# Sharing PSUM banks in the global attention: transposes four to a bank with the diagonal among them, products and splits of two query blocks together

## The chip, the core and the metric

The program runs on one core of a Trainium2 chip. The metric is device time in microseconds (us) from one execution of the whole program; less is better. TensorE is called PE, its weight loads PEld, VectorE DVE, ScalarE ACT, GpSimd POOL, and SP issues most DMAs.

## The reference

Three layers follow each other for 4 batches of 576 tokens, all in float32. First a banded attention over 8 heads (window 64, head width 64). Then a mixture of 4 attention experts, each causal over all 576 tokens, weighted by a gate that keeps 2 of the 4. Then a mixing layer with an angle, a token mix and a channel mix. The change is in the middle one:

```python
for e in range(E):                       # E = 4 experts, Hd = 64
    q = x @ wq[e]
    k = x @ wk[e]
    v = x @ wv[e]
    scores = scale * (q @ k.transpose(0, 2, 1))
    scores = np.where(causal, -1000000000.0, scores)
    scores = scores - scores.max(-1, keepdims=True)
    a = np.exp(scores)
    a /= a.sum(-1, keepdims=True) + 1e-09
    ye = a @ v @ wo[e]
    ...                                  # out += (gate weight of e) * ye
```

## The kernel before

Work is written as Python generators, one for each part: `phase_a` (banded attention of a batch), `qk` and `vg_gates` (projections and gates), `attn` (the causal attention of two experts, the part that is changed), `wo` (its output projection), `theta`, `mix`, `channel` (the last layer) and loaders of weights. `merge` interleaves a few of them by hand-set weights (the numbers in `KN`), and a scheduler then orders each engine's instructions. It works by a simulated timeline, so on an engine the order may differ from the order of emission: an instruction that is ready can come before one that was written earlier. Each engine then runs its own list strictly in that order.

`attn(b, ep)` handles batch b and the experts 2·ep and 2·ep+1, so it runs 8 times. It goes through five blocks of queries, t = 0 to 4: block 0 has 64 queries, the others have 128 each, and block t sees `QW[t]` keys. For each block it computes scores on PE (L382, L384), takes mask and maximum on DVE (L386) and exponentials on ACT (L391), and scales the weights on DVE or POOL (L403). The weights against earlier keys lie in `pn`, and those of both experts against the last 64 keys, the diagonal, side by side in `pd`. The weights are then transposed on PE, 128 columns at a time, into PSUM: up to four blocks (two key groups by two experts) into one bank `bpt` (L414), and the diagonal into a bank `bdt` of its own (L420). ACT or DVE copies each bank into the SBUF tile `pT`, called `bpT` in the profile (L416, L418 for `bpt`, L422, L424 for `bdt`; the lists `KN["BC"]` and `KN["BD"]` choose the engine). `pT` has two buffers, used in turn by successive query blocks.

The products with the values go into a third bank, `o`. Those of one expert against 128 keys (L429) have a weight tile of 64 columns and write one half of the partitions, and the two experts' halves are side by side in the array; the profile writes such a shape as `128*64`. The diagonal's product for both experts (L433) uses all 128 columns, `128*128`. A float32 product is two instructions in the trace, so block t has 4·t instructions of L429 and two of L433. Block t = 0 has only L433. `split` then moves `o` to SBUF as a high part (`oh`, a cast on ACT, L87) and a rest (`ol`, a subtraction on DVE, L90), which `wo` reads later.

The banks of `bpt`, `bdt` and `o` all come from `tbank`, two banks with the tag `tb`; in the last batch every third request goes to another tag, `ta`, with one bank. `phase_a` has products of 64 columns as well (`ao`, L260).

Of the kernel before, what the change touches and what calls it, by code (L numbers as in the profile page):

```python
# [21 lines left out]
P = 128  # L22
B, H, S, D = 4, 8, 576, 64
# [17 lines left out]
def f32(ap):  # L41
    return ap.bitcast(F32)
# [15 lines left out]
def kernel(ctx, tc, qT, kT, vw, consts, w_in, w_o, w_th, w_tk, w_ch, outT):  # L58
    nc = tc.nc
# [5 lines left out]
    ident, ma1, ma0 = (cst[:, P * i : P * i + P] for i in range(3))  # L65
# [12 lines left out]
    def bank(shape, tag, name):  # L78
        return ps.tile(shape, F32, tag=tag, bufs=BANKS[tag], name=name)
# [5 lines left out]
    def split(dst_h, dst_l, src, eng_h, eng_l):  # L85
        if eng_h is nc.scalar:
            nc.scalar.copy(out=dst_h, in_=src)  # L87
        else:
            eng_h.tensor_copy(out=dst_h, in_=src)
        eng_l.tensor_sub(out=dst_l, in0=src, in1=f32(dst_h))  # L90
# [70 lines left out]
    VD = [bp.tile([P, 5, 2, D], F32, tag=f"VD{i}", name=f"VD{i}") for i in range(2)]  # L161
# [187 lines left out]
    def tbank(b, shape, name):  # L349
        nt[0] += 1  # L350
        return bank(shape, "ta" if b == B - 1 and nt[0] % KN["TB"] == 0 else "tb", name)

    def attn(b, ep):
        vg, gw = VG[b], GW[b]
        for i in range(2):
            e = 2 * ep + i
            pool_mul(VD[ep][64 * i : 64 * i + 64, :, i, :], vg[0:64, :, e * D : (e + 1) * D], 1.0)
        oh = bp.tile([P, S], F32R, tag="oh", bufs=3, name=f"oh{b}{ep}")
        ol = bp.tile([P, S], F32R, tag="ol", bufs=3, name=f"ol{b}{ep}")
        O[b, ep] = (oh, ol)  # L360
        for t in range(5):
            w = QW[t]
            q0 = 0 if t == 0 else 64 + P * (t - 1)
            m = 64 if t == 0 else P
            mo = S - P if t == 0 else S - w
            if b == B - 1 and ep == 1 and t % 3 == 1:
                pn = rp.tile([P, 2, S], F32, tag="bmsx", name=f"bms{b}{ep}{t}")
            else:
                pn = bp.tile([P, 2, S], F32, tag="bms", bufs=2, name=f"bms{b}{ep}{t}")
            ss = sums(1, BS)  # L370
            sm = bp.tile([P, 2], F32, tag="bsm", bufs=4, name=f"bsm{b}{ep}{t}")
            pd = bp.tile([P, 2, 64], F32, tag="bpd", bufs=2, name=f"bpd{b}{ep}{t}")
            for i in range(2):
                e = 2 * ep + i
                n = f"{b}{e}{t}"
                qs, ka = QS[b, e], KA[b, e]
                ms = pn[:, i]
                cuts = [(0, w)] if w <= 512 else [(0, w // 2), (w // 2, w)]
                nm = bp.tile([P, 2], F32, tag="bnm", bufs=6, name=f"bnm{n}")
                for ci, (a, z) in enumerate(cuts):  # L380
                    s = sbank(b, [P, 512], f"bs{n}{a}")
                    nc.tensor.matmul(s[:m, : z - a], qs[:, q0 : q0 + m], ka[:, a:z],  # L382
                                     start=True, stop=False)
                    nc.tensor.matmul(s[:m, : z - a], qs[:, q0 : q0 + m], KL[e][:, a:z],  # L384
                                     start=False, stop=True)
                    nc.vector.tensor_tensor_reduce(  # L386
                        out=ms[:m, a:z], in0=s[:m, : z - a], in1=mb[:m, mo + a : mo + z],
                        scale=-0.125, scalar=nm[:m, 0:1] if ci else 3.0e38,
                        op0=ALU.add, op1=ALU.min, accum_out=nm[:m, ci : ci + 1],
                    )  # L390
                ex = nc.scalar.activation(out=ms[:m, :w], in_=ms[:m, :w], func=AF.Exp,  # L391
                                     bias=nm[:m, ci : ci + 1], scale=-1.0, accum_out=ss[:m, i, 0:1])
                if (b, ep, t, i) == (3, 1, KN["LT"], 1):
                    late[0] = ex
            nc.vector.tensor_reduce(out=sm[:m], in_=ss[:m], op=ALU.add, axis=AX.X)
            nc.vector.reciprocal(out=sm[:m], in_=sm[:m])
            for i in range(2):
                eng = nc.gpsimd if (False, i == 1 and t < 4, i == 1, t >= 2, i == 1 or t >= 3, True)[KN["SC"][2 * b + ep]] else nc.vector
                ms = pn[:, i]
                for dst, src in ((pd[:m, i], ms[:m, P * t : w]), (ms[:m, : P * t], ms[:m, : P * t])):  # L400
                    if src.shape[1] == 0:
                        continue
                    eng.tensor_scalar(out=dst, in0=src, scalar1=sm[:m, i : i + 1],  # L403
                                      scalar2=gw[:m, t, 2 * ep + i : 2 * ep + i + 1],
                                      op0=ALU.mult, op1=ALU.mult)
            yield 0.25 * (t + 1)
            pT = bp.tile([P, 5, 2, P], F32, tag="bpT", bufs=2, name=f"bpT{b}{ep}{t}")
            for j0 in range(0, t, 2):
                jn = min(2, t - j0)
                pt = tbank(b, [P, 2, 2, P], f"bpt{b}{ep}{t}{j0}")  # L410
                for jj in range(jn):
                    j = j0 + jj
                    for i in range(2):
                        nc.tensor.transpose(pt[:, jj, i, :], pn[:, i, P * j : P * j + P], ident)  # L414
                if (0, j0 == 2, t % 2, 1)[KN["BC"][b]]:
                    nc.vector.tensor_copy(out=pT[:, j0 : j0 + jn], in_=pt[:, :jn])  # L416
                else:
                    nc.scalar.copy(out=pT[:, j0 : j0 + jn], in_=pt[:, :jn])  # L418
            pt = tbank(b, [P, P], f"bdt{b}{ep}{t}")
            nc.tensor.transpose(pt[:, :m], pd[:m].rearrange("p h d -> p (h d)"), ident[:m, :m])  # L420
            if KN["BD"][b] == 0 or KN["BD"][b] == 1 and t % 2:
                nc.vector.tensor_copy(out=pT[:, t, 0, :m], in_=pt[:, :m])  # L422
            else:
                nc.scalar.copy(out=pT[:, t, 0, :m], in_=pt[:, :m])  # L424
            o = tbank(b, [P, P], f"o{b}{ep}{t}")
            for j in range(t):
                for i in range(2):
                    e = 2 * ep + i
                    nc.tensor.matmul(  # L429
                        o[64 * i : 64 * i + 64, :m], vg[:, j, e * D : (e + 1) * D],  # L430
                        pT[:, j, i, :m], start=(j == 0), stop=False,
                    )
            nc.tensor.matmul(o[:, :m], VD[ep][:, t].rearrange("p h d -> p (h d)"), pT[:, t, 0, :m], start=(t == 0), stop=True)  # L433
            split(oh[:, q0 : q0 + m], ol[:, q0 : q0 + m], o[:, :m], nc.scalar, nc.vector)
            yield 0.4 * (t + 1)

    def wo(b):
# [290 lines left out]
```

## Time and profile before

| what | value |
|---|---|
| median of 3 runs | 536.91 us (536.49 to 537.25) |
| the profiled execution, its time | 536.14 us |
| span of its instructions | 534.3 us |
| PE busy | 511.4 us |
| PEld busy | 479.2 us |
| DVE, ACT, POOL busy | 326.4, 331.2, 303.9 us |

The span is from the first to the last instruction of the trace; 1.84 us of the execution's time lie around it. Busy time of PE counts from the start of each matmul to its modelled end, and neighbours overlap, so it says little about how tightly they follow each other; starts do. The calls of `attn` lie between about 64 and 314 us; before them are batch 0's banded attention and projections, after them the last layer.

### The profile page before, as it was taken

What the parts mean: (1) busy time and instruction counts of PE and PEld (TensorE: products, weight loads), DVE (VectorE), ACT (ScalarE), POOL (GpSimd) and SP (SyncE); (2) the same over time, 40 slices, a digit from 0 to 9 for tenths busy, and PEclk for the clock granted to TensorE, in tenths of its full rate; (3) what the DMA queues carried; (4) which work ended last, traced back from release to release, by engine and by line L of the source; (5) the groups of instructions that cost most, each with busy time, mean ns of one, the idle gap of its engine ahead of it and who ended that gap; (6) DMA issues with size and microseconds to landing.
All of it is one profiled execution on the core that took longest, in us unless ns stands there. A gap on an engine that the chain in (4) does not pass through costs nothing.

```text
span 534.3 us, 12401 instructions
## 1 busy us (share of the span) xinstructions
PE 511.4 (96%) x4372; PEld 479.2 (90%) x4372; DVE 326.4 (61%) x1268; ACT 331.2 (62%) x1049; POOL 303.9 (57%) x463
## 2 busy tenths in 40 slices
PE   6879999999999999999699999999999999999997
PEld 5769988899988899989588889999999999999997
DVE  5786798757777578746888958462335434443312
ACT  6977687856868667868587977560545235432410
POOL 5697798735866763165866567880484316541420
PEclk9999999999999999999799999999999999999999
DMA  8764233321324331102103211002000100011002
GB/s 272 212 192 133 67 117 93 93 77 31 117 77 136 92 119 31 31 16 90 46 1 110 90 60 62 18 1 78 14 2 1 57 34 1 1 45 46 0 1 90
DMA packets 20798, 36.80 MB, mean 69 GB/s; under 512 B 2304, under 2 KB 13056, under 8 KB 20736
## 3 DMA queue, kind: packets, MB, share of 16 engines
q1 hardware_dynamic: 19008, 31.55, 19.1%
q10 hardware_dynamic: 1728, 4.46, 2.5%
q8 instruction: 35, 0.57, 0.5%
q14 instruction: 27, 0.22, 0.1%
HBM read 31.28 MB, written 4.72 MB: 67 GB/s over the span
## 4 chain that ended last, share of the span: by engine, by line
PE 76%; ACT 7%; DVE 6%; POOL 4%; DMA 3%; issue 3%; SPq 1%; ACTq 0%; POOLq 0%; DVEq 0%
PE y L95 7%; PE y L94 7%; PE y L93 7%; PE as L225 5%; PE c L94 3%; PE c L93 3%; PE c L95 3%; PE ao L260 3%; PE o L429 3%; PE th L95 3%; PE th L93 3%; PE th L94 3%; PE qk L93 3%; PE bpt L414 2%; PE qk L94 2%
## 5 line engine op out<-in xcount | busy, mean ns | idle before, releaser
L90 POOL TENSOR_TENSOR z<-zf,z 128x256 fp32r<-128x256 f32 x72 | 53.0, 751 | 88.6 <-ACT z L87 86.6
L93 PE MATMUL y<-wkh,z 128*128 128x288 f32 x288 | 85.7, 299 | 0.0
L94 PE MATMUL y<-wkl,z 128*128 128x288 f32 x288 | 85.0, 296 | 0.0
L95 PE MATMUL y<-wkh,z 128*128 128x288 f32 x288 | 83.6, 297 | 0.0
L238 ACT ACTIVATE ams<-ams,anm 128x128 f32<-128x128 f32 x144 | 56.7, 397 | 6.1 <-DVE anm L230 5.8
L245 POOL TENSOR_TENSOR ams<-ams,arc 128x384 f32<-128x384 f32 x48 | 40.2, 840 | 27.8 <-DVE arc L244 7.5
L94 PEld LDWEIGHTS y<-wkl,z 128*128 128x128 f32 x288 | 54.1, 188 | 0.0
L93 PEld LDWEIGHTS y<-wkh,z 128*128 128x128 f32 x288 | 54.1, 188 | 0.0
L95 PEld LDWEIGHTS y<-wkh,z 128*128 128x128 f32 x288 | 53.5, 188 | 0.0
L391 ACT ACTIVATE bms<-bms,bnm 64x64 f32<-64x64 f32 (+4 forms) x80 | 44.8, 561 | 11.7 <-DVE bnm L386 10.6
L87 ACT CAST z<-zf 128x256 fp32r<-128x256 f32 x72 | 27.5, 404 | 38.8 <-DVE zf L513 16.7
L225 PE MATMUL as<-kt,QD 128*128 128x128 f32 x288 | 43.2, 288 | 5.0 <-ACT QD L220 3.6
L82 POOL TENSOR_SCALAR QD<-qt 64x192 f32<-64x192 f32 x72 | 39.9, 554 | 12.1 <-PE as L225 8.9
L513 DVE TENSOR_TENSOR zf<-xk,ang 128x256 f32<-128x256 f32 x64 | 25.1, 418 | 32.8 <-ACT ang L500 21.3
L225 PEld LDWEIGHTS as<-kt,QD 128*128 128x128 f32 x288 | 36.8, 195 | 8.8 <-ACT QD L220 3.7
L498 ACT ACTIVATE ang<-ang 128x256 f32<-128x256 f32 x36 | 14.5, 416 | 48.4 <-DVE ang L497 48.4
L230 DVE CUSTOM_DVE_ANT_0 ams<-as,cst 128x128 f32<-128x128 f32 x144 | 34.4, 284 | 5.4 <-PE apt L250 4.5
L93 PE MATMUL th<-wth,cx 128*128 128x256 f32 x128 | 36.5, 285 | 1.2 <-DVE ang L497 1.2
L386 DVE CUSTOM_DVE_ANT_0 bms<-bs,mb 64x64 f32<-64x64 f32 (+4 forms) x80 | 32.4, 423 | 6.9 <-PE bs L384 4.8
L94 PE MATMUL th<-wtl,cx 128*128 128x256 f32 x128 | 36.0, 282 | 0.0
L90 POOL TENSOR_TENSOR cu<-x2T,cu 128x288 fp32r<-128x288 f32 x32 | 25.5, 822 | 18.1 <-ACT cu L87 18.1
L95 PE MATMUL th<-wth,cx 128*128 128x256 f32 x128 | 35.6, 284 | 0.0
(194 smaller groups left out, 1714.3 us busy)
## 6 DMA issues: line engine op xcount, KB each, us to landing
vt<-in_dram SPq DMA_DIRECT2D x48, 192.0 KB, 2.5
kt<-in_dram SPq DMA_DIRECT2D x16, 320.0 KB, 3.4
qt<-in_dram SPq DMA_DIRECT2D x16, 288.0 KB, 3.1
out_dram<-x2T SPq DMA_DIRECT2D x32, 144.0 KB, 1.8
w64k<-in_dram SPq DMA_DIRECT2D x5, 576.0 KB, 3.8
w64k<-in_dram ACTq DMA_DIRECT2D x4, 576.0 KB, 3.9
w64t<-in_dram SPq DMA_DIRECT2D x4, 512.0 KB, 4.2
w64c<-in_dram ACTq DMA_DIRECT2D x8, 256.0 KB, 2.8
```

The source lines that it names most:

```text
L82: nc.gpsimd.tensor_scalar(out=out, in0=in_, scalar1=by, scalar2=1.0, op0=ALU.mult, op1=ALU.mult)
L87: nc.scalar.copy(out=dst_h, in_=src)
L90: eng_l.tensor_sub(out=dst_l, in0=src, in1=f32(dst_h))
L93: nc.tensor.matmul(out, wh, xh, start=first, stop=False)
L94: nc.tensor.matmul(out, wh, xl, start=False, stop=False)
L95: nc.tensor.matmul(out, wl, xh, start=False, stop=last)
L225: nc.tensor.matmul(s[:, i, :], QD[g][:, i], kt[:, 64 * blk : 64 * blk + 128], start=True, stop=True)
L230: nc.vector.tensor_tensor_reduce(out=ms[:, i, :], in0=s[:, i, :], in1=ma0 if (g == 0 and i == 0) else ma1, scale=-0.125, scalar=3.0e38, op ...
L238: nc.scalar.activation(out=ms[:, i, :], in_=ms[:, i, :], func=AF.Exp, bias=nm[:, i : i + 1], scale=-1.0, accum_out=sm[:, i, 0:1],)
L245: nc.gpsimd.tensor_mul(out=ms, in0=ms, in1=rc.unsqueeze(2).to_broadcast([P, 3, P]))
L386: nc.vector.tensor_tensor_reduce(out=ms[:m, a:z], in0=s[:m, : z - a], in1=mb[:m, mo + a : mo + z], scale=-0.125, scalar=nm[:m, 0:1] if ci ...
L391: ex = nc.scalar.activation(out=ms[:m, :w], in_=ms[:m, :w], func=AF.Exp, bias=nm[:m, ci : ci + 1], scale=-1.0, accum_out=ss[:m, i, 0:1])
```

## The change

Inside `attn` alone:

- The diagonal's transpose no longer has a bank of its own. All the transposes of a query block are put into one list, the diagonal last, and go four to a bank; each bank is copied to `pT` at once. Where the diagonal shares a bank, the copy follows the rule of the other blocks; where it is left over alone (t = 0, 2, 4), it follows the diagonal's rule.
- Query blocks 1 and 2, and 3 and 4, now share one bank for their products, which come when the transposes of the second have been copied. In the first block of a pair the diagonal's product, over all 128 columns, is put first and starts the bank; in the second it stays last. Block 0 is alone as before.
- The split runs once for a pair, over 256 columns.

```diff
+        done = []
         for t in range(5):
...
             pT = bp.tile([P, 5, 2, P], F32, tag="bpT", bufs=2, name=f"bpT{b}{ep}{t}")
-            for j0 in range(0, t, 2):
-                jn = min(2, t - j0)
-                pt = tbank(b, [P, 2, 2, P], f"bpt{b}{ep}{t}{j0}")
-                for jj in range(jn):
-                    j = j0 + jj
+
+            blocks = [(j, i) for j in range(t) for i in range(2)] + [None]
+            pf = pT.rearrange("p j i q -> p (j i) q")
+            for k0 in range(0, len(blocks), 4):
+                part = blocks[k0 : k0 + 4]
+                pt = tbank(b, [P, 4, P], f"bpt{b}{ep}{t}{k0}")
+                for k, blk in enumerate(part):
+                    if blk is None:
+                        nc.tensor.transpose(pt[:, k, :m], pd[:m].rearrange("p h d -> p (h d)"), ident[:m, :m])
+                    else:
+                        j, i = blk
+                        nc.tensor.transpose(pt[:, k, :], pn[:, i, P * j : P * j + P], ident)
+                if part == [None]:
+                    on_dve = KN["BD"][b] == 0 or KN["BD"][b] == 1 and t % 2
+                else:
+                    on_dve = (0, k0 == 4, t % 2, 1)[KN["BC"][b]]
+                (nc.vector.tensor_copy if on_dve else nc.scalar.copy)(
+                    out=pf[:, k0 : k0 + len(part), :m], in_=pt[:, : len(part), :m])
+
+            done.append((t, m, q0, pT))
+            if t in (1, 3):
+                yield 0.4 * (t + 1)
+                continue
+            o = tbank(b, [P, len(done), P], f"o{b}{ep}{t}")
+
+            for k, (u, m, _, pT) in enumerate(done):
+                head = k == 0 and len(done) == 2
+                full = (o[:, k, :m], VD[ep][:, u].rearrange("p h d -> p (h d)"), pT[:, u, 0, :m])
+                if head:
+                    nc.tensor.matmul(*full, start=True, stop=False)
+                for j in range(u):
                     for i in range(2):
-                        nc.tensor.transpose(pt[:, jj, i, :], pn[:, i, P * j : P * j + P], ident)
...
-            pt = tbank(b, [P, P], f"bdt{b}{ep}{t}")
-            nc.tensor.transpose(pt[:, :m], pd[:m].rearrange("p h d -> p (h d)"), ident[:m, :m])
...
-            o = tbank(b, [P, P], f"o{b}{ep}{t}")
-            for j in range(t):
-                for i in range(2):
-                    e = 2 * ep + i
-                    nc.tensor.matmul(
-                        o[64 * i : 64 * i + 64, :m], vg[:, j, e * D : (e + 1) * D],
-                        pT[:, j, i, :m], start=(j == 0), stop=False,
-                    )
-            nc.tensor.matmul(o[:, :m], VD[ep][:, t].rearrange("p h d -> p (h d)"), pT[:, t, 0, :m], start=(t == 0), stop=True)
-            split(oh[:, q0 : q0 + m], ol[:, q0 : q0 + m], o[:, :m], nc.scalar, nc.vector)
+                        e = 2 * ep + i
+                        nc.tensor.matmul(
+                            o[64 * i : 64 * i + 64, k, :m], vg[:, j, e * D : (e + 1) * D],
+                            pT[:, j, i, :m], start=(j == 0 and not head), stop=(head and j == u - 1),
+                        )
+                if not head:
+                    nc.tensor.matmul(*full, start=(u == 0), stop=True)
+            q0 = done[0][2]
+            split(oh[:, q0:w], ol[:, q0:w], o.rearrange("p k q -> p (k q)")[:, : w - q0], nc.scalar, nc.vector)
+            done.clear()
             yield 0.4 * (t + 1)
```

## Rows read from the trace of the kernel before

**Rows 1.** The page: span, busy time by engine, and the clock granted in 40 slices.

```profile
span 534.3 us, 12401 instructions
PE 511.4 (96%) x4372; PEld 479.2 (90%) x4372; DVE 326.4 (61%) x1268; ACT 331.2 (62%) x1049; POOL 303.9 (57%) x463
PEclk9999999999999999999799999999999999999999
```

**Rows 2.** Busy us of each engine by stretch: stretch, length, engines (instructions), clock, DMA.

```profile
64.00:248.00 184.00, 180.67 (x1735) 161.93 (x1735) 134.88 (x635) 138.98 (x496) 111.23 (x192) 1.00 0.26 77
248.00:264.00 16.00, 11.32 (x72) 9.88 (x71) 13.77 (x40) 11.17 (x29) 13.51 (x16) 0.88 0.31 98
264.00:314.00 50.00, 47.62 (x378) 42.84 (x378) 40.39 (x127) 41.90 (x112) 32.23 (x37) 0.97 0.17 59
```

**Rows 3.** PE's timeline around a run of 4: start, us, engine, line, names, count.

```profile
134.51 0.28 PE L95 MATMUL x<-oh,wol 128*128 128x256 f32 x1
134.63 0.27 PE L420 MATMUL bdt<-cst,bpd 128*128 128x128 f32 x1
134.83 0.44 PE L429 MATMUL o<-bpT,vg 128*64 128x128 f32 x4
135.20 0.40 PE L382 MATMUL bs<-KA,QS 128*128 128x288 f32 x1
135.44 0.29 PE L384 MATMUL bs<-KL,QS 128*128 128x288 f32 x1
135.57 0.28 PE L93 MATMUL x<-oh,woh 128*128 128x256 f32 x1
```

**Rows 4.** PE's timeline around a run of 12.

```profile
104.48 0.27 PE L420 MATMUL bdt<-cst,bpd 128*128 128x128 f32 x1
104.69 0.88 PE L429 MATMUL o<-bpT,vg 128*64 128x128 f32 x12
105.49 0.40 PE L93 MATMUL qk<-x1h,wih 128*128 128x288 f32 x1
105.73 0.29 PE L94 MATMUL qk<-x1l,wih 128*128 128x288 f32 x1
105.86 0.29 PE L95 MATMUL qk<-x1h,wil 128*128 128x288 f32 x1
```

**Rows 5.** PE's timeline: the first and the last of 35 runs of L429.

```profile
69.99 0.44 PE L429 MATMUL o<-bpT,vg 128*64 128x128 f32 x4
...
310.05 1.09 PE L429 MATMUL o<-bpT,vg 128*64 128x128 f32 x16
```

**Rows 6.** Costliest groups, by shape: busy us, mean ns, idle before it.

```profile
L90 DVE TENSOR_TENSOR ol<-o,oh 128x128 fp32r<-128x128 f32 x32 | 9.1, 283 | 4.1 <-ACT oh L87 3.9
L87 ACT CAST oh<-o 128x128 fp32r<-128x128 f32 x32 | 8.4, 263 | 8.4 <-PE o L433 8.2
L445 ACT COPY x2T<-x 128x256 f32<-128x256 f32 x16 | 5.7, 372 | 2.1 <-PE x L95 2.0
L416 DVE COPY bpT<-bpt 128x256 f32<-128x256 f32 x6 | 2.5, 418 | 1.0 <-PE bpt L414 1.0
L418 ACT COPY bpT<-bpt 128x256 f32<-128x256 f32 x10 | 3.7, 370 | 0.2
L424 ACT COPY bpT<-bdt 128x128 f32<-128x128 f32 x24 | 6.3, 264 | 1.2 <-PE bdt L420 1.2
L255 ACT COPY apv<-apt 128x384 f32<-128x384 f32 x33 | 15.7, 477 | 6.3 <-PE apt L250 6.1
```

**Rows 7.** PE's timeline at the end of the starved stretch.

```profile
264.33 0.47 PE L93 MATMUL x<-oh,woh 128*128 128x320 f32 x1
264.59 0.47 PE L94 MATMUL x<-ol,woh 128*128 128x320 f32 x1
...
268.44 0.31 PE L93 MATMUL x<-oh,woh 128*128 128x320 f32 x1
268.59 0.31 PE L94 MATMUL x<-ol,woh 128*128 128x320 f32 x1
```

**Rows 8.** Busy us by stretch, within the last call of attn.

```profile
290.00:300.00 10.00, 8.83 (x73) 7.70 (x74) 9.64 (x29) 9.92 (x23) 6.65 (x7) 1.00 0.49 174
```

More of the change, by code (lines that the diff above doesn't have):

```diff
@@ L407, in attn @@
             pT = bp.tile([P, 5, 2, P], F32, tag="bpT", bufs=2, name=f"bpT{b}{ep}{t}")
-            for j0 in range(0, t, 2):
-                jn = min(2, t - j0)
-                pt = tbank(b, [P, 2, 2, P], f"bpt{b}{ep}{t}{j0}")
-                for jj in range(jn):
-                    j = j0 + jj
-                    for i in range(2):
-                        nc.tensor.transpose(pt[:, jj, i, :], pn[:, i, P * j : P * j + P], ident)
[L415 to L418, printed above, removed]
@@ L419, in attn @@
-            pt = tbank(b, [P, P], f"bdt{b}{ep}{t}")
-            nc.tensor.transpose(pt[:, :m], pd[:m].rearrange("p h d -> p (h d)"), ident[:m, :m])
[L421 to L424, printed above, removed]
-            o = tbank(b, [P, P], f"o{b}{ep}{t}")
-            for j in range(t):
-                for i in range(2):
-                    e = 2 * ep + i
-                    nc.tensor.matmul(
-                        o[64 * i : 64 * i + 64, :m], vg[:, j, e * D : (e + 1) * D],
-                        pT[:, j, i, :m], start=(j == 0), stop=False,
-                    )
```

## The prediction

> **What bounds the kernel now.** I read the page first. PE is the fullest engine by far, and the clock is granted in full except in one slice of the attention [rows 1]. So a change pays only where it shortens what PE does, or fills a time in which PE waits.
>
> The second view is busy time by stretch [rows 2]. The attention calls fall into three. From 64 to 248 us PE is busy 180.67 of 184 us while DVE and ACT have a quarter of their time free: PE sets the pace. From 248 to 264 PE has work for 11.32 of 16 us and waits for DVE, ACT and POOL, which are converting weights. From 264 to 314 PE is at 47.62 of 50, with DVE and ACT near full in places: from 290 to 300 they are busy 9.64 and 9.92 of 10 [rows 8]. 12 of the 16 pairs (2 in each of 8 calls) belong to the first three batches, whose products end by 248 us; the last batch's 4 pairs lie in the third stretch.
>
> PE's busy time hides how tightly its instructions follow each other, so the third view is its timeline, and there the starts. Rows 3 and 4 show two runs of the 64-column products with the same kind of neighbour on both sides. In the run of 4, L429 starts 0.20 us after the transpose ahead of it; that transpose had come 0.12 after its own forerunner. The run takes 0.37 to the next instruction's start, and that one 0.24 to its follower, which then takes 0.13 [rows 3]. In the run of 12 the same steps are 0.21, 0.80, 0.24 and 0.13 [rows 4]. Eight more instructions cost 0.43, so 0.054 each, and four of them account for 0.22 of the 0.37. The run therefore carries 0.15 inside it, 0.08 ahead of it and 0.11 behind it that the number of products does not explain: **0.34 us for going into the 64-column shape and out again**. No engine is named as awaited there; the busy view counts all of it as work.
>
> The Trainium skill (Perfetto Trace Analysis, "Identifying the Most-Contended Engine") holds that matmul busy time is a poor measure of headroom and that the busy share of weight loads should be read in its place. In the stretch to 248 us the first leaves 3.3 us and the second 22 us [rows 2]; were the first the limit, that stretch could give 3.3 us at most and the sum below would come to 533.8; by the second it can give the whole term. The starts side with the page.
>
> **The change, part by part.**
>
> *Products of two blocks together.* The number of products stays. What changes is how often PE goes in and out of the 64-column shape. There are 35 runs of L429 now [rows 5], for 8 calls times 4 blocks = 32, so three were split by other work. With the first block's full-width product ahead of its 64-column ones, and the second's behind, the 64-column products of both are neighbours: 16 runs, or 19 if three are split again. That saves 16 × 0.34 = 5.4 us of PE time. The bounds: 0 if the scheduler tears every pair apart, 19 × 0.34 = 6.5 if no run is split. I take 5.4, because only 3 of 32 are split now and all products of a pair wait for the same bank and for copies made shortly before.
>
> *Transposes four to a bank.* The same 200 transposes. They lose no shape change, as both kinds are full width. The copies fall from 11 to 9 in each call, so from 88 to 72. On ACT a block of 256 columns (370 ns) and a diagonal (264) become one copy of 384, for which the nearest row is 477 [rows 6]: 157 ns less. On DVE 256 columns take 418; 384 are bounded by that below and by 418 + 283 above. In batches 1 and 3 a diagonal moves from DVE to its neighbours' engine. Counted over all calls this is about 1 us less of ACT and 1 to 2 less of DVE.
>
> *One split for two blocks.* 40 casts become 24, 40 subtractions 24. A cast of 128 columns takes 263 ns, a copy of 256 from PSUM 372; so two casts of 526 become one of about 372. A subtraction of 283 becomes one of between 283 and 566; the cast's growth, 1.4 times, gives about 400. So 16 × 0.15 = 2.5 us come off ACT and as much off DVE. To 248 us both are worth nothing: PE's own work covers them. If that cover were gone they would be worth up to about 3.5 us each. In the last stretch the four pairs give some 0.6 us on each of two full engines.
>
> *What is later.* The products of blocks 1 and 3 wait for the block after. `wo` reads them in the next stage, so seven of the eight calls don't feel it. In the last call the 12 products of block 3 (0.65 us) move to the end, and the last cast and subtraction are 0.25 us longer together; PE has other products of the last layer there, so I charge 0.3 us.
>
> *Banks.* A call asks for 12 banks of `tb` in place of 16. The Trainium skill (Perfetto Trace Analysis, "Matmuls") advises that independent product groups rotate through different banks, so that emptying one overlaps the next one's products; the change does the reverse. By rows, that costs at most the longer emptying: a cast and a subtraction of about 0.79 us in place of 0.55 [rows 6], 0.24 for each of 16 pairs, 3.8 us if all of it is bare. Today's waits of the cast for the products are ACT's, not PE's, so I take nothing, and keep 3.8 for a rival.
>
> *The sum.* 12 pairs where PE sets the pace: 12 × 0.34 = −4.1. Four in the last stretch: −1.4, half of it lost to DVE and ACT: −0.7. The starved stretch from 248 to 264 hangs on the last banded attention through memory that it reuses, so it moves forward with PE; for what its transfers don't follow I give back 0.6. The tail: +0.3. Together −3.9. From the profiled execution's 536.14 (1.84 around a span of 534.3) that is 532.2; this execution lies 0.77 below the median of 536.91, so on the median's scale **533.0**.
>
> **The rivals.**
>
> *No gain (17 in 100, two ways).* In the first way the pairs come apart: the first block's weights are transposed long before the second's, and the scheduler may issue its products as soon as they are ready. If a quarter stays together, 4 × 0.34 = −1.4 and the tail: 535.8. For it speaks that L429 already stands apart from its own L433 in both runs shown [rows 3, 4]; against it that the bank is asked for only after the second block's. In the second way, the bank rule above holds everywhere: −3.9 + 3.8, so 536.8.
>
> *Slower: the held buffer (20 in 100).* `pT` has two buffers, and blocks 1 and 2 now hold both until the pair's products are done. Block 3's first copy needs the buffer of block 1. On ACT, which runs in order, the exponentials of the next block and the copies of the banded attention are queued behind that copy, and PE waits for them. Its price is a run of 12, 0.15 + 12 × 0.054 = 0.80 us, once in each call: 6.4 us if all 8 are bare, which gives 536.9 − 3.9 + 6.4 = 539.4. With five bare waits the gain is gone; from seven on it is measurably slower. Against it: block 3's scores and exponentials lie between, and PE has other work to issue in the first stretch.
>
> *More gain (13 in 100).* In the starved stretch PE then runs at half speed for a while, at 1.2 GHz: L93 to L94 takes 0.26 us at 264.33 and 0.15 at 268.44 [rows 7]. Some 15 matmuls between 263.8 and 267.1 stand so; at 0.11 more they are 1.7 us. If the new order keeps PE fed there, this and the 1.0 of savings that I gave back are won: 533.0 − 2.7 = 530.3.
>
> **How the numbers follow.** The forecast itself has 50 in 100, with a range of its own from 531.5 (the whole 5.4 passes on) to 534.4 (10 pairs pass, less the 0.6 and the 0.3). About 0.2%, 1.1 us, is what a measurement of this kernel can tell from no change. Faster: 50 + 13 + 7 of the no-gain cases = 70. Same: the other 10. Slower: 20. The range has to take in the no-gain cases and half of the slow ones, and most of the high gain: 530.5 to 538.5, leaving out about 5 below and 10 above.
>
> **What would show it.** Right: about 16 to 20 runs of L429 on PE's timeline, of 12 and 28, with a full-width product on each side; a cast and a subtraction of 256 columns, 16 of each; PE's time between 64 and 248 us shorter by some 4 us while its idle time stays. Wrong: runs of 4, 8, 12 and 16 as before; or fewer runs, but longer idle times of PE put down to `bpT` copies or exponentials; or a second stretch of half clock. The prediction fails if the new order of instructions starves PE by more than 4 us anywhere in the last batch.

## The result: slower, 540.11 us

The changed kernel takes 540.11 us (median of 7, 539.54 to 544.0) against 536.75 (median of 7, 535.52 to 537.25) for the kernel before on the same chip: 1.0087 times as long, 95% interval 1.0062 to 1.0111. The forecast was 533.0, with a range from 530.5 to 538.5.

The page of the changed kernel, lines as in [rows 1]. PE is busy 0.5 us less, ACT 2.9 and DVE 1.7 less, and the span is 4.0 longer:

```profile
span 538.3 us, 12363 instructions
PE 510.9 (95%) x4372; PEld 479.6 (89%) x4372; DVE 324.7 (60%) x1244; ACT 328.3 (61%) x1025; POOL 305.2 (57%) x463
PEclk9999999999999999999799999999999999999999
```

Busy time by stretch, as in [rows 2]. To 248 us PE now has 5.4 us without work where it had 3.3, from 248 to 264 3.6 where it had 4.7, and from 264 to 314 3.7 where it had 2.4. The windows are the same, but the work in them has moved by some us:

```profile
64.00:248.00 184.00, 178.61 (x1717) 160.47 (x1716) 130.75 (x620) 134.25 (x471) 110.53 (x193) 1.00 0.26 76
248.00:264.00 16.00, 12.45 (x91) 11.63 (x90) 13.15 (x30) 11.34 (x29) 12.82 (x15) 0.97 0.36 111
264.00:314.00 50.00, 46.28 (x367) 41.92 (x366) 42.78 (x130) 41.31 (x107) 32.91 (x37) 0.94 0.18 59
```

The groups of copies and splits (busy us, mean ns, idle time before). They are as long as the prediction took them from [rows 6]: a copy of 384 columns 475 ns on ACT (forecast 477), a cast of 256 370 (372), a subtraction 417 (400):

```profile
L90 DVE TENSOR_TENSOR ol<-o,oh 128x256 fp32r<-128x256 f32 x16 | 6.7, 417 | 3.3 <-ACT oh L87 2.9
L87 ACT CAST oh<-o 128x256 fp32r<-128x256 f32 x16 | 5.9, 370 | 7.0 <-PE o L447 6.9
L425 ACT COPY bpT<-bpt 128x384 f32<-128x384 f32 x10 | 4.7, 475 | 0.2 <-PE bpt L417 0.2
L425 DVE COPY bpT<-bpt 128x384 f32<-128x384 f32 x6 | 3.3, 551 | 0.7 <-PE bpt L417 0.6
```

PE's timeline shows both fates of a pair; L442 is now the line of the 64-column products, L438 the full-width product at the head, L447 the one at the end. First a pair that came apart: the first block's 4 products run at 97.39, the second block's 8 only at 101.04, and the scheduler has put banded attention, projections and scores between them. Then a pair of 12 in one run, as the change means it [rows 3, 4]:

```profile
97.07 0.39 PE L438 MATMUL o<-bpT,VD 128*128 128x128 f32 x2
97.39 0.44 PE L442 MATMUL o<-bpT,vg 128*64 128x128 f32 x4
97.76 0.94 PE L225 MATMUL as<-kt,QD 128*128 128x128 f32 x6
98.62 0.57 PE L260 MATMUL ao<-apv,vt 128*64 128x64 f32 x12
...
101.04 0.66 PE L442 MATMUL o<-bpT,vg 128*64 128x128 f32 x8
101.62 0.49 PE L447 MATMUL o<-bpT,VD 128*128 128x128 f32 x2
```

```profile
140.68 0.49 PE L438 MATMUL o<-bpT,VD 128*128 128x128 f32 x2 [0.24 <-ACT bpT L425]
141.10 0.88 PE L442 MATMUL o<-bpT,vg 128*64 128x128 f32 x12
141.91 0.40 PE L383 MATMUL bs<-KA,QS 128*128 128x288 f32 x1
```

There are 28 runs of L442 in this trace where the forecast had 16, or 19; before it was 35 [rows 5]. Six of the 16 pairs run as one; five of the eight pairs of blocks 1 and 2 come apart between the blocks, as at 97.39; the other five are interrupted elsewhere.

### Where the time went

Busy time hides PE's spacing, so I added up starts. For each PE instruction I took the time to the next start, less the pitch that its kind has among its like (0.133 us for 288 columns, as in [rows 4]). What is over is called *idle* where the profile has an idle time, however short, ahead of the next instruction, *shape* where exactly one of the two has the 64-column products' shape (those of the banded attention, `ao`, included), and *other* else; a time at half clock falls under *other*. Stretch A runs from the 46th transpose of the banded attention to its 118th (61 to 197 us in the kernel before), stretch B from there to the 72nd instruction of the last layer's token mix that is called `y<-wkh,z` (333 us). B holds the last batch and the end of batch 2. Behind B all kernels take 200.5 to 201.4 us. Ahead of A lie 61.0 to 63.7, and there one and the same list of PE differs from run to run (61.75 and 63.44 in two traces of the changed kernel's list), so nothing is read from it. *Runs* counts the stretches of 64-column instructions of both attentions in PE's list. All in us, each from one trace; the first column is the median of the timed runs, which for the rows e1 to e18 were made on five chips. The ratios further down compare each kernel with the kernel before on its own chip, where that takes from 535.95 to 537.04:

```
kernel                             time   runs | A len  idle shape other | B len   idle shape other
before                             536.75  75  | 135.58  4.77  8.50  7.94 | 136.86 10.58  5.22  7.47
after                              540.11  68  | 135.91  6.43  7.79  7.90 | 140.19 13.62  4.27  8.11
e1  transposes only                537.27  78  | 136.21  4.97  9.18  7.68 | 135.61  9.20  5.37  7.44
e2  products only                  541.58  71  | 135.48  6.44  7.51  7.73 | 141.32 14.98  4.94  7.21
e3  change, second block first     537.93  63  | 135.11  5.99  7.29  7.46 | 137.82 13.22  3.58  7.42
e4  products put off, own banks    541.25  78  | 135.76  4.38  9.26  8.03 | 141.27 13.02  5.27  9.08
e5  e4 with free buffers           544.25  78  | 136.28  4.88  9.26  8.05 | 143.39 13.76  5.36 10.38
e6  change with free buffers       541.41  68  | 136.57  7.37  7.67  7.73 | 140.99 13.68  4.26  8.87
e7  e3 with free buffers           542.22  63  | 135.06  5.87  7.29  7.52 | 142.63 15.27  3.58 10.18
e8  before with free buffers       536.72  74  | 135.94  5.06  8.50  8.00 | 136.42 11.04  5.01  6.78
e11 e3 in three batches            536.18  68  | 135.64  6.59  7.20  7.48 | 136.43 10.98  4.72  7.14
e12 e3, blocks 3 and 4 only        537.26  67  | 135.99  6.62  7.45  7.54 | 137.39  9.59  4.17 10.03
e13 shared bank, products at once  544.26  82  | 137.51  6.31  8.44  8.38 | 143.41 11.68  6.55 11.59
e14 e12 in three batches           534.99  69  | 135.19  5.88  7.44  7.50 | 134.35  9.31  4.41  7.03
e15 e2, second block first         533.23  64  | 133.64  5.83  7.47  7.35 | 133.54  7.61  3.95  6.98
e16 e2, bank only when all ready   541.98   -  | 138.11  5.89  7.58  9.36 | 138.84 12.48  3.93  7.92
e17 change, the same               543.26   -  | 137.54  5.48  7.72  9.07 | 141.24 12.90  3.99  9.85
e18 e15 with another order         540.74  63  | 134.35  5.89  7.26  7.56 | 140.96 12.83  4.06  9.73
```

From before to after, shape changes fall by 1.66 us in both stretches together, idle time grows by 4.70 and the rest by 0.60. Of the 3.66 us that A and B lose, B alone loses 3.33; the three terms give it 2.73, and the other 0.60 is work that moved across the border from A. The same two lists of instructions were traced once more, as e9 and e10: A takes 135.21 and 137.06 there, B 135.09 and 139.82. So one trace's length is sure to some 2 us, while the idle time of B came back within 0.3 us.

### The profile page after: what moved, and what is told of

Its sections match the earlier page's. It is cut to its first block, busy times and chain, and to the rows that moved or that the text cites. A ratio compares the mean times of both kernels' runs of the same rounds, so it can differ in the third digit from the quotient of the medians.

```text
span 538.3 us, 12363 instructions
## 1 busy us (share of the span) xinstructions
PE 510.9 (95%) x4372; PEld 479.6 (89%) x4372; DVE 324.7 (60%) x1244; ACT 328.3 (61%) x1025; POOL 305.2 (57%) x463
## 4 chain that ended last, share of the span: by engine, by line
PE 75%; DVE 11%; ACT 6%; issue 2%; POOL 2%; DMA 2%; SPq 1%; ACTq 0%; POOLq 0%; DVEq 0%
PE y L95 7%; PE y L94 7%; PE y L93 7%; PE as L225 4%; PE o L442 3%; PE c L93 3%; PE c L94 3%; PE c L95 3%; PE bpt L420 3%; PE ao L260 3%; PE qk L93 3%; PE th L93 3%; PE th L95 3%; PE th L94 3%; PE qk L94 2%; PE qk L95 2%
## 5 line engine op out<-in xcount | busy, mean ns | idle before, releaser
L575 DVE SCALAR_TENSOR_TENSOR x2T<-c,x2T 128x288 f32<-128x288 f32 x32 | 14.5, 457 | 34.3 <-PE c L95 34.2
```

## The experiments

### Which part of the change

*e1*: only the transposes four to a bank, products and splits as before.

```diff
-            for j0 in range(0, t, 2):
-                jn = min(2, t - j0)
-                pt = tbank(b, [P, 2, 2, P], f"bpt{b}{ep}{t}{j0}")
...
+            blocks = [(j, i) for j in range(t) for i in range(2)] + [None]
+            for k0 in range(0, len(blocks), 4):
+                part = blocks[k0 : k0 + 4]
+                pt = tbank(b, [P, 4, P], f"bpt{b}{ep}{t}{k0}")
...
```

> Only the transposes' half of the change: four to a bank with the diagonal, copied together; products and splits stay one block to a bank. Its order has 78 runs of 64-column products of both attentions (before 75, after 68), so the shape changes alone give +3 x 0.34 = +1.0 us on 536.75. Theory of the order (the instruction order that came out of the list starves PE here and there, and no part of the change owns that): 537.8, with 2 us of scatter either way. Theory of the held products (putting off the first block's products holds its buffer and delays what is queued behind): nothing is put off here, so 536 to 538. Theory of the mixed banks (a bank with the diagonal waits for the slowest of its blocks, and the score tiles come free later): most of the loss is here, 540 or more.

*e2*: only products and splits of two blocks together, transposes as before.

```diff
+            done.append((t, m, q0, pT))
+            if t in (1, 3):
+                yield 0.4 * (t + 1)
+                continue
+            o = tbank(b, [P, len(done), P], f"o{b}{ep}{t}")
```

> Only the products' half: two blocks' products in one bank with one split; transposes and copies as before. 71 runs of 64-column products, so the shape changes alone give -4 x 0.34 = -1.4 us: 535.4. Theory of the order: 535.4 with 2 us either way. Theory of the held products: the whole loss is here, 540 or more. Theory of the mixed banks: 535 to 536.

*e3*: the change, with the second block's products ahead of the first's. The first block's copies are old by then, so nothing should come between the two.

```diff
-            for k, (u, m, _, pT) in enumerate(done):
-                head = k == 0 and len(done) == 2
+            for k, (u, m, _, pT) in reversed(list(enumerate(done))):
+                head = k == 1
```

> The change with the products of each pair in the other order: the second block's, which are ready last, go first, so that the scheduler finds all of them ready at once. 63 runs in place of the change's 68, 19 of them of the global attention: the number that the prediction counted on. By shape changes it is 5 x 0.34 = 1.7 us under the changed kernel's 540.1: 538.4, and 12 x 0.34 = 4.1 under the kernel before if nothing else moves: 532.7. Theory of the order: between these two, with 2 us either way. Theory of the held products and theory of the mixed banks: both stay in, so 538 to 540.

*e4*: the kernel before, in which the products of blocks 1 and 3 come only behind the transposes of blocks 2 and 4, each with its own bank and split.

```diff
+            done.append((t, m, q0, pT))
+            if t in (1, 3):
+                yield 0.4 * (t + 1)
+                continue
+            for u, m, q0, pT in done:
+                o = tbank(b, [P, P], f"o{b}{ep}{u}")
...
```

> The kernel before, but the products of blocks 1 and 3 come after the copies of blocks 2 and 4, each block still with its own bank and split. Nothing is won: 78 runs. It puts off the products alone. Theory of the held products: 540 or more. Theory of the order: 536.75 + 1.0 = 537.8, with 2 us either way. Theory of the mixed banks: 536 to 538.

Measured: e1 537.27 (ratio 1.0011, 0.9996 to 1.0026), e2 541.58 (1.0094, 1.0077 to 1.0111), e3 537.93 (1.0023, 1.0002 to 1.0045), e4 541.25 (1.0089, 1.0071 to 1.0108). So the transposes cost nothing by themselves, and the loss comes with the products. Putting them off, with the order that comes of it, is enough for all of it: e4 shares no bank and no split and is as slow as e2. Nearly all of e4's loss lies in B (+4.41 of +4.59).

### Do the weights' buffers hold up the next block?

The rival that came closest in time was the `pT` buffer that blocks 1 and 2 hold. e5, e6, e7 and e8 give blocks 0 and 1 a buffer of their own (the tiles are cut to 9 groups to make room), in e4, in the change, in e3 and in the kernel before, so that block 3 never waits for block 1.

```diff
-            pT = bp.tile([P, 5, 2, P], F32, tag="bpT", bufs=2, name=f"bpT{b}{ep}{t}")
+            if t < 2:
+                pf = bp.tile([P, 3, P], F32, tag="bpTa", name=f"bpT{b}{ep}{t}")
+            else:
+                pf = bp.tile([P, 9, P], F32, tag="bpT", bufs=2, name=f"bpT{b}{ep}{t}")
```

> The kernel with the products put off (541.25 us), with the held buffer taken away: blocks 0 and 1 get a small buffer of their own for the transposed weights, blocks 2, 3 and 4 take turns in the two others, so that block 3's copies never wait for the products of blocks 1 and 2. Same arithmetic. Theory of the held buffer (the copies of block 3 wait on ACT or DVE until the pair's products are done): the loss goes, 536.7 + 3 runs x 0.34 = 537 to 538. Theory of the missing filler (PE has lost the products of block 1 as work to do while block 2's exponentials are made, whatever the buffers): 540 to 542. Theory of the order: no forecast nearer than 537 to 542.

> The changed kernel (540.1 us) with the same free buffers. 68 runs of 64-column products against 75 before: -2.4 us of shape changes. Theory of the held buffer: 534.4 to 536. Theory of the missing filler: 539 to 541.

> The change with the second block's products first (537.9 us) and the free buffers. 63 runs. Theory of the held buffer: 532.7 to 535, the forecast of the prediction. Theory of the missing filler: 537 to 539, since the products are put off as before.

> Control: the kernel before with the free buffers and nothing else. All theories: 536.75, less 0.34 for one run fewer; if it is over 1 us faster, the two buffers already held the kernel before, and e5 to e7 are to be read against this one.

Measured: 544.25 (1.0123, 1.009 to 1.0156), 541.41 (1.0077, 1.0048 to 1.0106), 542.22 (1.0089, 1.0056 to 1.0122) and 536.72 (1.0006, 0.9985 to 1.0027). Not one became faster, and the theory of the held buffer falls. e5 and e7 also lie above what the missing filler gave. e7 is a surprise: the same products in the same runs as e3 (63 runs, shape 7.29 and 3.58 in both), and 4 us slower, all of it in B. Of the 4.81 us there 2.05 are idle time and 2.76 *other*: e7's trace has a second stretch at half clock, from 277.0 to 280.4 us, where e3's has one in all of B.

### Is it one order of instructions, or any?

e9 and e10 multiply the weights by which `merge` interleaves the attention by 0.9, in the kernel before and in the changed one.

```diff
-'AT': [12.51, 2.36, 85.51, 5.66, 48.01, 55.86, 30.7, 4.07]
+'AT': [11.26, 2.12, 76.96, 5.09, 43.21, 50.27, 27.63, 3.66]
```

> Control for the scatter of orders: the kernel before, with the weights that merge gives to the attention calls multiplied by 0.9. Nothing else changes; about a tenth of PE's list comes in another order, with the same 75 runs. Theory of the order (any new order costs, since this one is the best of many): 538.5 to 541, like the change. Theory of the missing filler: nothing is put off, so 535.5 to 538.

> The changed kernel with the same weights times 0.9 (68 runs as in the change). Theory of the order: anything between 536 and 542; if it comes under 537, the change's loss was one unlucky order. Theory of the missing filler: 539 to 542, as every kernel so far that puts the products off without joining all runs.

Measured: 536.55 (1.0005, 0.9987 to 1.0023) and 541.75 (1.0108, 1.0067 to 1.0149). They decide nothing: in both traces all 4,372 PE instructions stand in the order that they had without the edit. They are repeats of the measurement.

### Only part of the pairs

e11 is e3 with pairs in the first three batches alone, e12 is e3 with only blocks 3 and 4 as a pair, e14 has both limits.

```diff
-            if t in (1, 3):
+            if b < B - 1 and t in (1, 3):       # e11
+            if t == 3:                          # e12
+            if b < B - 1 and t == 3:            # e14
```

> Where the loss lies: transposes four to a bank everywhere, pairs (second block first) in batches 0 to 2, single blocks in batch 3, where PE is the one that waits. 68 runs. Theory of the missing filler: PE has other work in batches 0 to 2, so only the last batch pays: the main stretch as in e3 (182.6 us), the tail as in e1 (88.0), so 1.8 us under the kernel before: 534 to 535.5. Theory of the order: 535 to 540.

> Pairs (second block first) of blocks 3 and 4 alone in all batches, blocks 1 and 2 single; 67 runs. It puts off 8 times 12 products and not 8 times 4. Theory of the missing filler: the larger share of the filler is gone, so as slow as or slower than e3 (537.9): 538 to 541. Theory of the order: 535 to 540, no sign.

> A version for gain: transposes four to a bank, pairs of blocks 3 and 4 alone (second block first) and only in batches 0 to 2. 69 runs. From e12's main stretch (181.1 us against 182.3 before) and e1's tail (88.0 against 90.2), 3.4 us less: 533 to 534.5 if stretches add up, 536 if the tail of e1 was chance.

Measured: 536.18 (0.9994, 0.9973 to 1.0014), 537.26 (1.0024, 1.0005 to 1.0043) and 534.99 (0.9959, 0.9936 to 0.9982). With the last batch left alone, B is no longer than before (136.43 and 134.35 against 136.86), and e14 beats the kernel before. e11 and e12 miss what the missing filler gave, one above it and one below.

### Do PE's waits come from a missing filler, or from a bank taken too early?

In the changed kernel the first blocks' products start 81 us in all after their copies were there, and 4.67 of PE's 13.87 us without work between 64 and 316 us lie in those times: work that was ready and was not in the list. But these times are 32% of that stretch and hold 34% of its idle time, so the waits don't gather in them. In B they are 37 of 140 us and hold 1.99 of the 10.66 us without work, and from 250 to 330 us 0.57 of 8.82. In B, then, filling them all would have saved less than the 3 us by which its idle time grew. e13 has the shared bank and the shared split, but issues each block's products at once, with the old transposes.

```diff
+            if t in (0, 1, 3):
+                q1, o = q0, tbank(b, [P, 1 if t == 0 else 2, P], f"o{b}{ep}{t}")
+            k = 0 if t in (0, 1, 3) else 1
...
-            split(oh[:, q0 : q0 + m], ol[:, q0 : q0 + m], o[:, :m], nc.scalar, nc.vector)
+            if t not in (1, 3):
+                split(oh[:, q1:w], ol[:, q1:w], o.rearrange("p k q -> p (k q)")[:, : w - q1], nc.scalar, nc.vector)
```

> Transposes as before; blocks 1 and 2, and 3 and 4, share a bank and one split, but the products of the first are issued at once, as in the kernel before. No runs are joined: 82 runs against 75, which by shape changes costs 7 x 0.24 to 0.34 = 1.7 to 2.4 us. The bank stays taken through the second block, so the transposes have one bank only. Theory of the missing filler: nothing is put off, so 536.5 + about 2 = 538 to 539. Theory of the banks: worse than every other, 541 or more, since the bank is held three times as long as in the change.

e15 is e2 with the second block's products first, the edit of e3 on the old transposes.

> The products' half alone (541.6 us) with the second block's products first: 64 runs against 71. By shape changes 7 x 0.24 to 0.34 = 1.7 to 2.4 less: 539 to 540. If the order of the two blocks matters by more than the shape changes (it is what took e3 to 537.9), 537 to 538.5.

Measured: e13 544.26 (1.0124, 1.008 to 1.0168), e15 **533.23 (0.9917, 0.9888 to 0.9947)**, faster than both kernels and than both of its forecasts. So the filler can't be all: e13 puts nothing off and is slow, e15 puts off the same products as e2 and is 8.35 us faster. What went with these five was how long the products' bank is held, from a pair's (or block 0's) first product to the end of its split: 192 us in all in e13 (1.7 times the change's, not three times), 110 in the changed kernel, 101 in e2, 88 in e3, 77 in e15. `tb` has two banks, so the transposes have one meanwhile (in the last batch every third request goes elsewhere). e16 and e17 put that to the test: e2 and the change, first block first, with a tiny product at the head of each pair that reads a column of every group of the *second* block's copies. The next product overwrites it; the bank can't be taken before all is ready.

```diff
                 if head:
+                    ready = done[1][3].rearrange("p j i q -> p (j i) q")[:, : 2 * t + 1, 0]
+                    nc.tensor.matmul(o[:, 0, : 2 * t + 1], full[1], ready, start=True, stop=True)
                     nc.tensor.matmul(*full, start=True, stop=False)
```

> The kernel of e2 (products of two blocks in one bank, first block first, old transposes) with one tiny product more at the head of each pair: it reads a column of every copied group of the SECOND block into the same bank and is overwritten by the next product, so the bank can't be taken before the second block's copies are there. 16 such products cost some 1 to 2 us of PE. Theory (the bank of the pair is taken too early, while the second block's copies are still to come, and the transposes have one bank meanwhile): the time a bank is held falls from 101 us in all to below 85, PE's idle time falls, and the time comes near e15's: 533 to 537 us. Rival (the early bank is harmless, e15 gained by its order of instructions in another way): 541 to 544 us, e2 plus the products.

> The changed kernel with the same tiny product at the head of each pair. Theory: held time falls from 110 us to below 95, the time falls from 540 to near e3's with the products' cost, 536.5 to 539 us. Rival (early bank harmless): 541 to 543.

e18 is e15 with the weights of e9.

> The kernel of e15 (products of two blocks in one bank, second block's first, old transposes) with the weight of the attention in the interleaving multiplied by 0.9, which changes the list of instructions elsewhere (the kernel before didn't change its time by that). If e15's gain is the mechanism's: 531 to 535.5 us. If e15 was a lucky list: 536 to 541.

Measured: e16 541.98 (1.0094, 1.0073 to 1.0115), e17 543.26 (1.0127, 1.0105 to 1.0149), e18 540.74 (1.0073, 1.0054 to 1.0091). All three landed where the rival had put them, or just above.

In e16 the bank is held 90 us instead of 101 and PE's idle time is 3.05 us less than in e2; in e17 96 instead of 110, and 1.67 less. But the tiny products were dearer than thought: in e16's timeline L438 takes 0.13 us ahead of L439, 2.1 for 16, and *other* grew by 2.34 us in e16 and 2.91 in e17. Less idle time was paid for with about as much work, and the bank was not held as briefly as the theory had wanted (below 85 and 95 us), so these two don't separate the early bank from the rest; that it makes the change slow is not shown. Against it stand e7 and e18, which hold the bank 86 and 85 us in all, less than e3, and take 542.22 and 540.74.

```profile
142.70 0.28 PE L438 MATMUL o<-bpT,VD 128*128 128x5 f32 x2
142.83 0.47 PE L439 MATMUL o<-bpT,VD 128*128 128x128 f32 x2
143.23 0.88 PE L443 MATMUL o<-bpT,vg 128*64 128x128 f32 x12
144.04 0.49 PE L448 MATMUL o<-bpT,VD 128*128 128x128 f32 x2
```

e18 is the plainer answer. Its weights did change the list: matched by names and shapes, 4,071 of 4,372 PE instructions can be read in the same order in both, so some 300 have moved. Its products run in 63 runs, its shape changes cost what e15's do (11.32 against 11.42 us), A is 0.7 us longer, and B is 7.4 us longer: 5.2 more idle and 2.75 more *other*, with a second stretch at half clock from 301.2 us on, right behind a wait of 2.18 us. So e15's time belongs to its order of instructions, not to the second block's going first.

PE's idle times of at least 0.5 us in its timeline from 196 to 342 us, in full (start, us, engine, line, names, and in brackets the idle time and what ended it; line numbers differ from kernel to kernel). The changed kernel:

```profile
206.34 0.40 PE L93 MATMUL qk<-x0h,wih 128*128 128x288 f32 x1 [1.06 <-DVE QS L290]
253.47 0.38 PE L93 MATMUL vg<-wih,x1h 128*128 128x260 f32 x1 [0.81 <-ACT vg L307]
261.13 0.36 PE L383 MATMUL bs<-KA,QS 128*128 128x192 f32 x1 [2.25 <-DVE bnm L387]
266.01 0.63 PE L93 MATMUL x<-oh,woh 128*128 128x320 f32 x1 [0.90 <-ACT x2T L461]
277.88 0.40 PE L93 MATMUL qk<-x1h,wih 128*128 128x288 f32 x1 [0.57 <-ACT x2T L461]
283.79 0.30 PE L420 MATMUL bpt<-cst,bms 128*128 128x128 f32 x1 [0.91 <-DVE bms L404]
300.30 0.42 PE L93 MATMUL x<-oh,woh 128*128 128x320 f32 x1 [1.26 <-DVE bnm L387]
316.00 0.88 PE L93 MATMUL x<-oh,woh 128*128 128x256 f32 x4 [1.21 <-ACT oh L87]
```

The kernel before:

```profile
254.56 0.38 PE L93 MATMUL qk<-x1h,wih 128*128 128x288 f32 x1 [0.58 <-DVE KL L293]
257.26 0.24 PE L382 MATMUL bs<-KA,QS 128*64 128x64 f32 x1 [0.86 <-POOL KA L82]
259.37 0.39 PE L93 MATMUL x<-oh,woh 128*128 128x320 f32 x1 [1.02 <-DVE KL L293]
263.39 0.61 PE L93 MATMUL x<-oh,woh 128*128 128x320 f32 x1 [1.55 <-DVE QS L290]
297.26 0.39 PE L93 MATMUL th<-wth,cx 128*128 128x256 f32 x1 [1.17 <-DVE ang L497]
312.85 0.73 PE L93 MATMUL x<-oh,woh 128*128 128x256 f32 x4 [0.73 <-ACT oh L87]
```

e15, and then e18:

```profile
253.04 0.42 PE L383 MATMUL bs<-KA,QS 128*64 128x64 f32 x2 [1.17 <-POOL KA L82]
256.54 0.37 PE L93 MATMUL qk<-x1h,wih 128*128 128x288 f32 x1 [1.18 <-DVE KL L293]
261.90 0.61 PE L93 MATMUL x<-oh,woh 128*128 128x320 f32 x1 [1.73 <-DVE QS L290]
```

```profile
201.01 0.37 PE L93 MATMUL qk<-x0h,wih 128*128 128x288 f32 x1 [1.10 <-DVE QS L290]
253.89 0.39 PE L93 MATMUL vg<-wih,x1h 128*128 128x260 f32 x1 [0.82 <-ACT vg L307]
261.51 0.36 PE L383 MATMUL bs<-KA,QS 128*128 128x192 f32 x1 [2.19 <-DVE bnm L387]
266.40 0.63 PE L93 MATMUL x<-oh,woh 128*128 128x320 f32 x1 [1.05 <-ACT x2T L460]
278.25 0.40 PE L93 MATMUL qk<-x1h,wih 128*128 128x288 f32 x1 [1.26 <-ACT x2T L460]
301.15 0.64 PE L93 MATMUL x<-oh,woh 128*128 128x320 f32 x1 [2.18 <-DVE bnm L387]
```

The starved stretch around 260 us is there in all four. What the changed kernel and e18 share beyond it are waits for the copies of the projections (`vg`, `x2T`) and for the score maxima (`bnm`) on ACT and DVE, five of at least 0.5 us in each, 5.79 and 7.50 us in all, which the kernel before and e15 don't have. None of them is a wait of the pair's products. They don't make a kernel slow by themselves: e11, as fast as the kernel before, has three of them too (`vg` 0.80, `bnm` 2.16, `x2T` 0.72 us).

The view of PE's waits from 197 to 342 us shows which kind grew (in total, times, longest; the changed kernel, then the kernel before, then e4):

```profile
PE bs L383 <- DVE bnm L387: 2.3, 1, 2.3
PE x L93 <- DVE bnm L387: 1.3, 1, 1.3
PE bpt L420 <- DVE ol L90: 0.2, 1, 0.2
```

```profile
PE bs L382 <- DVE bnm L386: 0.3, 1, 0.3
```

```profile
PE bs L383 <- DVE bnm L387: 2.3, 1, 2.3
PE o L436 <- DVE ol L90: 1.2, 1, 1.2
PE x L93 <- DVE bnm L387: 1.2, 1, 1.2
```

Waits ended by DVE's mask and maximum, `bnm`, go in B from 0.3 us to 3.5, about as much as its idle time grows; in the second traces of the two lists they are 1.0 and 3.4. Waits for the emptying of a products' bank, `ol`, are 0.2 us in the changed kernel (the view names waits of over 0.15 us). So PE's added waits end with DVE's work on the scores. That is where this order loses, not a rule: in B the `bnm` waits are 3.5 us in e4, 5.1 in e18 and none in e15, but e2 is slow with 1.4, and e11 and e14 are not slow with 2.5 and 2.2.

## Why the prediction was wrong, step by step

**What bounds the kernel: right.** PE does, and what PE does not save it waits.

**The price of a change of shape: too high; the number of runs: the first step that failed.** From e4 to e2, which differ in whether a pair shares its bank and split and in where the first block's diagonal product stands, 7 runs fewer in the list take off 2.08 us of shape time (14.53 to 12.45), 0.30 each; from before to after, again 7 fewer, 1.66, 0.24 each. The forecast was 0.34. But "I take 5.4, because only 3 of 32 are split now" counted on pairs that stay together, and the trace has 28 runs: in five pairs the scheduler issued the first block's products ahead of the second's with other work between, as the rival of pairs that come apart had it, and in five more other work came in elsewhere. This term is 1.66 us instead of 5.4. Where the second block goes first and most pairs stay whole (e3, e15, e18: 63 or 64 runs, 11 or 12 fewer) it is 2.3 to 2.9, some 0.2 a run, so even whole pairs would not have given 5.4.

**Copies, casts and subtractions: right in size, and worth nothing that a run shows.** For the copies e1 shows it by itself (1.0011); the shorter split was not tried without the products put off.

**What is later: the step that made the change slow.** "`wo` reads them in the next stage, so seven of the eight calls don't feel it" asked who reads the products, and not what PE, DVE and ACT then do in their place. The sum took PE's list to stay as it was, and has no term for a new order. I charged 0.3 us; e4, which does this and nothing else, costs 4.5, and in the changed kernel PE's idle time grows by 4.7. The loss lies in the last batch: where all pairs are put off there (after, e2 to e7, e15 to e18; without e10, which repeats after) B takes from 133.5 to 143.4 us, in ten of the eleven kernels 137.8 or more, with idle times of 12.5 to 15.3; where the last batch keeps its products where they were (before, e1, e8, e11, e14) it takes 134.4 to 136.9, with 9.2 to 11.0. The exception is e15. Its B is shortest of all, so putting off has no fixed price: it decides through the order that the scheduler finds. Of the 4,372 PE instructions, matched by names and shapes, 3,632 can be read in the same order before and after the change, so some 740 have moved. In the changed kernel the waits that grew most in the last batch are those that end with the score maxima on DVE; ready work that is missing from the list there (at most 1.99 of 10.66 us) and the emptying of the pair's bank (0.2 us) don't make up the growth by themselves. Why ten orders of eleven are worse in that batch, and what put-off work or a held bank does to the order that the scheduler finds, stays open.

**Banks: "I take nothing" holds for the waits that the profile names.** Of the waits of over 0.15 us, which the profile names, PE has 0.2 us in A and B for the emptying of a pair's bank, where the rival had 3.8 (the prediction's own 0.372 and 0.400 add up to 0.77, not 0.79, so 3.6). From e4 to e2 idle time grows by 4.02 us (17.40 to 21.42), while shape changes and other spacing give 4.25 back (14.53 to 12.45, 17.11 to 14.94), and the time is the same. The sign is what the rule of the Trainium skill (Perfetto Trace Analysis, "Matmuls") would give, that independent groups of products should rotate through banks. But the waits don't bear it out: PE's named waits for a bank's emptying are 1.2 us in e4, which rotates, and none in e2. The two lists also differ in order, and in B e4's trace is at half clock for longer (268.2 to 275.0 us against 267.1 to 270.5), so what the bank does to the order is open.

**The tail: about right.** The last wait of `wo` for its cast is 1.21 us at 316.00, 0.73 in the kernel before: 0.48 more, forecast 0.3. (The rival of more gain counts 1.0 us as given back where the sum gives back 0.6 for the starved stretch; it did not occur.)

**The slower rival had nearly the time, 539.4, but not the cause:** with free buffers the change takes 541.41. What came nearest is the last of the signs, that the prediction fails if the new order starves PE by more than 4 us in the last batch. It starves PE by 3.0 us in B and by 1.7 in A: the kind of loss was named, but it stayed under that mark, was not confined to the last batch and stood in no rival.

## What to carry to other kernels

Where a scheduler makes the order, an edit's price has two parts, its own sum (here 1.7 us) and what the reordering does (in B, in these kernels, from 3 us for to 7 us against, with some 2 us of scatter); a forecast that sums only the first should carry a range as wide as the second. Ask of a piece of work that is put off not only who reads it, but what its engine has to run in its place, in the batch where the other engines are full; e14, which leaves that batch alone, gains 0.4% in the one order that was tried. And a faster variant found in this way is credited to its mechanism only when another order of the same mechanism is fast too: e15 gains 0.8%, e18 loses 0.7%.

## What the hardware showed that I had not expected

One list of PE instructions is granted more or less clock from run to run, and the time largely goes with it: of the changed kernel's 7 runs, four take 539.54 to 540.11 us at a mean granted clock of 0.994 to 0.997, three 542.33 to 544.0 at 0.987 to 0.991. The list of the kernel before was traced once with a stretch at half clock, 1.2 of 2.4 GHz, from 260.3 to 267.1 us (mean granted clock from 260 to 267 us: 0.52), and once, as e9, with none in B: B takes 136.86 and 135.09 us, with nearly the same idle time, so that stretch cost some 1.8 us. The changed kernel's trace has one as long (263.0 to 269.8 us), so its loss is not the clock's. And the slowest variant, e13, has three (0.51 from 263 to 270 us, 0.57 from 297 to 301 and from 307 to 311); its *other* in B is 11.59 us against 7.47.
